# The product with w_out in 2x2 blocks with seven products, and stage weights that arrive one product at a time

## The chip, the cores and the metric

The kernel runs on one core of a Trainium2 chip. A core has five engines that run their own instruction streams: TensorE (PE in the profile; its weight loads are PEld), VectorE (DVE), ScalarE (ACT), GpSimd (POOL) and SyncE (SP), which here only issues DMAs. The metric is the time of one execution in microseconds on the device, as the median of several runs. Before the change it is 1204.18 us (three runs: 1200.9, 1204.18, 1206.41).

## The reference

Three layers run one behind the other on 4608 tokens of width 512:

```
out = softmax(q_c k_c^T / 8) v_c            # attention in chunks of 64, 8 heads
x   = relu(x[mask_e] @ w1[e]) @ w2[e]       # 8 experts, 576 tokens each, greedy routing
h   = max(max(x @ w1, x @ w2), x @ w3)      # last stage: w1, w2, w3 are 512 x 768
y   = h @ w_out                             # w_out is 768 x 512
```

The result is float32. Every matrix product of the last two layers is done in three matmuls, from a high and a low part of each operand: high by high, low weight by high and high weight by low.

## The kernel before

The attention runs first, then routing and the eight experts (one expert after another, 576 tokens each, transposed, so that tokens lie along the free axis), then the last stage. Order on each engine is the order in which the program's lines emit instructions; there is no scheduler behind it. Each engine works through its own list and waits at an instruction until what it reads and overwrites is ready.

The last stage takes the tokens in six blocks of 768 (the loop over `s`). In a block the product with w1, w2, w3 is done in 2x2 blocks of both operands with seven block products (`p1` to `p7`, the loop over `k`, nine groups per block). A block product is six matmuls of 384 columns (`product`), and sums of the 2x2 blocks come before it (`xprep`) and behind it (`best`, which also takes the maximum over the three matrices). The three banks are `px`, `py` and `pz`, two buffers each. The result h is split into a high part by ScalarE and a low part by VectorE (`hpart`, `low`).

Then `layer2` multiplies h by w_out for six tiles of 128 tokens, in the plain way: six parts of the inner dimension by three matmuls of 512 columns, 18 for a tile. Two of these tiles stand between the last products of the block, and `xprep` for the next block stands between the other four. ScalarE copies each tile's result out (`ot`), and GpSimd scatters it to the output rows with an indirect DMA.

The weights of a group lie in DRAM as wda (three products, 768 KB a group) and wdb (four products, 1024 KB). They are loaded whole, two groups at a time in two places each (`wload_a`, `wload_b`), as soon as the last product that uses the place is done. w_out is loaded and split with the experts' weights, as three chunks more at the end of their list (`NC = 8 * E + 3`, `want`). POOL's work in the last stage is the scatter alone.

Of the kernel before, what the change touches and what calls it, by code (L numbers as in the profile page):

```python
# [699 lines left out]
def kernel(ctx, tc, q, k, v, w_gate, w1, w2, m1, m2, m3, m_out, out, mark=lambda n: None):  # L700
# [26 lines left out]
    NC = 8 * E + 3  # L727
# [248 lines left out]
    XO, WA, WB, Y = {}, [], [], []  # L976

    def yload(b):
        for i, tag in enumerate(("aoh", "c64")):
            if b == 0:  # L980
                Y.append(P.tile([128, 2, 2 * TB], F32, name="yraw%d" % i, tag=tag))
            nc.sync.dma_start(Y[i], yd[256 * i:256 * i + 256, b * 2 * TB:(b + 1) * 2 * TB]
                              .rearrange("(a p) t -> p a t", p=128))

    def wload_a(g):
        if g < 9 * NS:
            if g < 2:
                WA.append(P.tile([128, 2, 3, 2, 128], F32R, name="wa%d" % g, tag=("xhi", "xlo")[g]))
            nc.sync.dma_start(WA[g % 2].rearrange("p c o h f -> p (c o h f)").bitcast(F32),
                              wda[g % 9 * 128:g % 9 * 128 + 128].rearrange("p c w -> p (c w)"))  # L990

    def wload_b(g):
        if g < 9 * NS:
            if g < 2:
                WB.append(P.tile([128, 2, 4, 2, 128], F32R, name="wb%d" % g, tag="raw%d" % g))
            nc.sync.dma_start(WB[g % 2].rearrange("p c o h f -> p (c o h f)").bitcast(F32),
                              wdb[g % 9 * 128:g % 9 * 128 + 128].rearrange("p c w -> p (c w)"))

    def xprep(*ops):

        b11, b12 = Y[0][:, :, :TB], Y[0][:, :, TB:]
        b21, b22 = Y[1][:, :, :TB], Y[1][:, :, TB:]
        src = {"b11": b11, "b21": b21, "b22": b22, "t1": T1, "t2": T2, "t3": b12, "t4": b21}
        for o in ops:
            mark("ysplit")
            sub = {"t1": None, "t2": None, "t3": (b22, b12), "t4": (b21, T2)}.get(o)
            if o == "t2":
                nc.vector.tensor_tensor(T1, b12, b11, op=OP.subtract)
                nc.vector.tensor_tensor(T2, b22, T1, op=OP.subtract)
            elif sub:  # L1010
                nc.vector.tensor_tensor(src[o], *sub, op=OP.subtract)
            if o not in XO:
                XO[o] = ring.tile([128, 2, 2, TB], F32R, name="x" + o, tag="chunk")
            nc.scalar.copy(XO[o][:, 0], src[o])
            nc.vector.tensor_tensor(XO[o][:, 1], src[o], XO[o][:, 0].bitcast(F32), op=OP.subtract)
# [9 lines left out]
    for r in range(E):  # L1025
        if r + 1 == E:
            for i in range(3):
                want(mo.rearrange("(a p) f -> p a f", p=128)[:, 2 * i:2 * i + 2, :], 2, 2 * i + 2)
# [6 lines left out]
        for f in range(0, 8, 2):  # L1035
            have(8 * r + f // 2 + 1)
            w = [x.rearrange("p (a f) -> p a f", a=4) for x in chunks[8 * r + f // 2]]
            for f, hf in ((f, 0), (f + 1, 0), (f, 1), (f + 1, 1)) if r + f == 0 else ((f, 0), (f, 1), (f + 1, 0), (f + 1, 1)):
# [26 lines left out]
                if r + 1 == E and not state["next"] and not Y and XH[r][2] == 5:  # L1065
                    yload(0)
# [18 lines left out]
        if r + 1 == E:  # L1085
            while state["next"]:
                convert_one()
            if not Y:
                yload(0)
            for g in range(2):  # L1090
                wload_a(g)
            TMP = P.tile([128, 6, TB], F32, name="tmp", tag="xg")
            T1, T2 = TMP[:, 0:2], TMP[:, 2:4]
        state["l1"] = False
        for d in range(4):
# [20 lines left out]
            if r + 1 == E:  # L1116
                if d == 0:
                    have(NC)
                    for g in range(2):
                        wload_b(g)  # L1120
                xprep(*(("b11", "t2", "b21"), ("t1", "t3"), ("t4",), ("b22",))[d])
# [4 lines left out]
    WO = [x for c in chunks[8 * E:] for x in [[y.rearrange("p (a f) -> p a f", a=2) for y in c]]]  # L1126
    HT = [P.tile([128, 3, 2, 2 * TB], F32R, name="h%d" % i, tag=t) for i, t in enumerate(("hhi", "hlo"))]
    CT = P.tile([128, 2, TB], F32, name="cmax", tag="cw", bufs=2)
    MX = P.tile([128, 2, 2, TB], F32, name="best", tag="pair")
    XB, YZ, U = {}, {}, {}  # L1130
    tt = nc.vector.tensor_tensor
    nct = [0]
    scat = []

    def hview(f):
        return HT[f // 3][:, f % 3]

    def product(g, dst, w, o, x, start, stop):
        mark("mmB")
        n = 0  # L1140
        for dc in range(2):
            for a, c in ((0, 0), (1, 0), (0, 1)):
                nc.tensor.matmul(dst, w[:, dc, o, a], XO[x][:, c, dc], start=start and n == 0, stop=stop and n == 5,  # L1143
                                 skip_group_check=True)
                n += 1

    def best(g, i, j, a, b=None):

        m = g % 3
        M = MX[:, i, j]  # L1150
        if m == 0:
            if b is None:
                nc.scalar.copy(M, a)
            else:
                tt(M, a, b, op=OP.add)
        elif b is None:
            tt(M, M, a, op=OP.max)
        else:
            c = CT[:, nct[0] % 2]
            nct[0] += 1  # L1160
            tt(c, a, b, op=OP.add)
            tt(M, M, c, op=OP.max)  # L1162
        if m == 2:
            nc.scalar.copy(hpart(g, i, j)[0], M)  # L1164

    def hpart(g, i, j):
        h = hview(2 * (g % 9 // 3) + 1 - i)
        return [h[:, x, j * TB:j * TB + TB] for x in range(2)]

    def low(g, i, j):  # L1170
        if g % 3 == 2:
            hi, lo = hpart(g, i, j)
            tt(lo, MX[:, i, j], hi.bitcast(F32), op=OP.subtract)
# [7 lines left out]
    def p6(g):  # L1181
        YZ[g] = [PS.tile([128, 512], F32, name=n)[:, :TB] for n in ("py", "pz")]
        product(g, YZ[g][0], WA[g % 2], 0, "t2", True, False)
# [3 lines left out]
    def p4(g):  # L1187
        product(g, YZ[g][0], WB[g % 2], 0, "t4", False, True)
        best(g, 1, 0, YZ[g][0], U[g, 1])

    def p3(g):
        product(g, YZ[g][1], WB[g % 2], 3, "b22", False, True)
        wload_b(g + 2)
        best(g, 0, 1, YZ[g][1], U[g, 2])

    def p2(g):
        product(g, XB[g], WA[g % 2], 2, "b21", False, True)
        wload_a(g + 2)
        best(g, 0, 0, XB[g])

    def p5(g):
        product(g, YZ[g][1], WB[g % 2], 1, "t1", True, False)

    def p7(g):
        product(g, YZ[g][0], WB[g % 2], 2, "t3", False, False)
        u3 = TMP[:, 4 + g % 2]
        tt(u3, YZ[g][0], U[g, 1], op=OP.add)
        best(g, 1, 1, YZ[g][1], u3)
# [3 lines left out]
    def layer2(t, fs):  # L1212
        if t not in PO:
            PO[t] = PS.tile([128, 512], F32, name="po")
        for f in fs:
            w, h = WO[f // 2], hview(f)
            mark("mmO")
# [3 lines left out]
        if fs[-1] != 5:  # L1221
            return
# [72 lines left out]
```

## Time and profile before

| | |
|---|---|
| runs | 1200.9, 1204.18, 1206.41 us; median 1204.18 |
| profiled execution | 1201.66 us; span in the trace 1199.9 us |
| mean granted TensorE clock | 0.989 of 2.4 GHz; 1.0 throughout the last stage |
| TensorE busy | 1170.7 us, 98% of the span |
| VectorE, ScalarE, GpSimd busy | 828.6, 413.2, 312.3 us |
| last stage | from 653.7 us to the end |

The trace gives, for each instruction, when it started, how long it took, and what the engine waited for before it. Matmuls overlap: one of 384 columns is recorded with 334 ns, but the next starts 173 ns behind it, so the distance between starts is what one costs. The same holds in a small way for VectorE and ScalarE.

### The profile page before, as it was taken

Reading aid. Unit: us, or ns where it says so; the run is one execution under the profiler, and the core shown is the slowest. Engines: PE = TensorE matmul, PEld = TensorE weight load, DVE = VectorE, ACT = ScalarE, POOL = GpSimd, SP = SyncE. Lnnn points to the kernel's source line nnn. Section 1 sums busy time; section 2 is a strip of 40 time slices with the busy share of each in tenths; the row PEclk is TensorE's granted clock in tenths of the full one; section 3 lists DMA queues with packets and bytes.
Section 4 is the critical chain, followed back from the end, with each engine's and each line's share of the span. In section 5 each row is a group of like instructions: output and inputs, shape, how many; then the busy total and the mean of one; then the engine's idle time right before and its main releaser. Section 6 shows DMA issues by size and latency. Waiting matters only on the chain.

```text
span 1199.9 us, 23581 instructions
## 1 busy us (share of the span) xinstructions
PE 1170.7 (98%) x9508; PEld 1095.3 (91%) x9508; DVE 828.6 (69%) x1660; ACT 413.2 (34%) x674; POOL 312.3 (26%) x507
## 2 busy tenths in 40 slices
PE   7999979999999999999999999999999999999998
PEld 5887847999999999999999998998998998998996
DVE  6898976788788888888753665664664664664661
ACT  5998822243333333325333113113113113113111
POOL 8433201011027463757771002002002002002002
PEclk8999978999999999999999999999999999999999
DMA  9999515273646566669755763773773773773651
GB/s 257 274 279 257 159 45 168 89 241 121 210 140 211 181 208 187 196 206 289 240 184 203 288 257 111 288 259 111 286 258 110 287 260 110 288 257 110 237 186 53
DMA packets 138828, 242.99 MB, mean 203 GB/s; under 512 B 30048, under 2 KB 101216, under 8 KB 131808
## 3 DMA queue, kind: packets, MB, share of 16 engines
q1 hardware_dynamic: 118608, 180.90, 46.2%
q0 software_dynamic: 14976, 51.13, 12.8%
q10 hardware_dynamic: 5136, 9.46, 2.3%
q8 instruction: 75, 1.23, 0.4%
q14 instruction: 33, 0.27, 0.1%
HBM read 195.05 MB, written 46.40 MB: 201 GB/s over the span
## 4 chain that ended last, share of the span: by engine, by line
PE 55%; issue 36%; POOL 3%; DVE 3%; SPq 1%; DMA 1%; ACT 1%; POOLq 1%; ACTq 0%; DVEq 0%
PE acc L1105 17%; PE acc L1050 16%; PE pX L181 3%; PE py L1143 2%; PE pT L115 2%; POOL out_dram L1227 2%; PE pS L132 2%; PE po L1219 2%; PE pA L168 2%; PE px L1143 2%; PE pz L1143 2%; PE pxt L821 1%; PE pY L199 1%; PE rp L553 1%; SPq L71 1%
## 5 line engine op out<-in xcount | busy, mean ns | idle before, releaser
L1105 PE MATMUL acc<-hhi,chunk 128*128 128x288 f32 x1024 | 209.9, 299 | 0.0
L1050 PE MATMUL acc<-xhi,chunk 128*128 128x288 f32 (+2 forms) x1024 | 206.4, 300 | 2.5 <-DVE chunk L768 1.3
L1227 POOL DMA_INDIRECT out_dram<-ot,ia x36 | 36.3, 1008 | 508.5 <-ACT ot L1225 507.9
L1050 PEld LDWEIGHTS acc<-xhi,chunk 128*128 128x128 f32 x1024 | 160.7, 188 | 3.7 <-DVE chunk L768 1.5
L1105 PEld LDWEIGHTS acc<-hhi,chunk 128*128 128x128 f32 x1024 | 162.9, 188 | 0.3
L1105 PE MATMUL acc<-hlo,chunk 128*128 128x288 f32 x512 | 150.8, 295 | 0.0
L1219 PE MATMUL po<-chunk,h 128*128 128x512 f32 x648 | 149.3, 390 | 0.0
L1219 PEld LDWEIGHTS po<-chunk,h 128*128 128x128 f32 x648 | 121.4, 188 | 24.8
L1050 PE MATMUL acc<-xlo,chunk 128*128 128x288 f32 (+2 forms) x512 | 143.1, 295 | 0.0
L1143 PE MATMUL px<-xb,wa 128*128 128x384 f32 x648 | 129.9, 334 | 0.7 <-ACT ys L1112 0.7
L1143 PE MATMUL py<-xt,wb 128*128 128x384 f32 x648 | 129.8, 334 | 0.0
L1143 PEld LDWEIGHTS px<-xb,wa 128*128 128x128 f32 x648 | 114.0, 188 | 1.3 <-ACT ys L1112 1.0
L1143 PEld LDWEIGHTS py<-xt,wb 128*128 128x128 f32 x648 | 114.1, 188 | 0.5
L1164 ACT CAST h<-best 128x384 fp32r<-128x384 f32 x72 | 37.0, 514 | 198.1 <-DVE best L1162 121.3
L1105 PEld LDWEIGHTS acc<-hlo,chunk 128*128 128x128 f32 x512 | 96.0, 188 | 0.0
L1050 PEld LDWEIGHTS acc<-xlo,chunk 128*128 128x128 f32 x512 | 93.4, 188 | 0.0
L768 DVE TENSOR_TENSOR chunk<-raw,chunk 128x1024 fp32r<-128x1024 f32 x67 | 86.0, 1289 | 7.6 <-ACT chunk L761 6.6
L1074 ACT ACTIVATE hhi<-acc 128x576 fp32r<-128x576 f32 (+1 forms) x66 | 41.9, 638 | 132.8 <-PE acc L1050 130.1
L798 POOL DMA_INDIRECT xg<-xd,idx x40 | 43.0, 1075 | 167.5 <-DVE ohe L688 88.7
L1179 ACT COPY tmp<-px 128x384 f32<-128x384 f32 x54 | 25.9, 479 | 146.2 <-PE px L1143 146.2
L761 ACT CAST chunk<-raw 128x1024 fp32r<-128x1024 f32 x67 | 69.6, 1046 | 8.6 <-ACT ys L1112 4.8
L1083 DVE SCALAR_TENSOR_TENSOR hlo<-acc,hhi 128x576 fp32r<-128x576 f32 (+1 forms) x66 | 48.3, 735 | 25.3 <-ACT hhi L1074 25.1
(222 smaller groups left out, 2047.9 us busy)
## 6 DMA issues: line engine op xcount, KB each, us to landing
wb<-wdb SPq DMA_DIRECT2D x54, 1024.0 KB
wa<-wda SPq DMA_DIRECT2D x54, 768.0 KB
raw<-in_moe_w_dram SPq DMA_DIRECT2D x64, 512.0 KB
xd<-x POOLq DMA_DIRECT2D x36, 256.0 KB
yd<-ys ACTq DMA_DIRECT2D x32, 288.0 KB
wdb<-pair POOLq DMA_DIRECT2D x18, 512.0 KB
yraw<-yd SPq DMA_DIRECT2D x12, 768.0 KB
ink<-in_k_dram SPq DMA_DIRECT2D x16, 512.0 KB
```

The costliest lines, as they stand in the source:

```text
L181: nc.tensor.matmul(PX[g][c * 64:(c + 1) * 64, hp, :], AT[g][:, hp, c * 64:c * 64 + 64], VB[u % 3][:, 2 * h + c, hp].rearrange("p s i -> p ...
L761: nc.scalar.copy(hi, raw)
L768: nc.vector.tensor_tensor(lo, raw, hi.bitcast(F32), op=OP.subtract)
L798: nc.gpsimd.indirect_dma_start(out=g, out_offset=None, in_=xd[:, :], in_offset=bass.IndirectOffsetOnAxis(ap=rt.idx[r][:, t:t + 1], axis=0))
L1050: nc.tensor.matmul(acc[:, hf, :tk.stop - tk.start], w[a][:, dc, o:o + 128], x[:, dc, tk], start=n == 0, stop=n == 11)
L1074: nc.scalar.activation(hv, src, AF.Relu)
L1083: nc.vector.scalar_tensor_tensor(lv, src, 0.0, hv.bitcast(F32), op0=OP.max, op1=OP.subtract)
L1105: nc.tensor.matmul(acc[:, hf, :288], w[a][:, f, :], x[:, f, tk], start=n == 0, stop=n == 23)
L1143: nc.tensor.matmul(dst, w[:, dc, o, a], XO[x][:, c, dc], start=start and n == 0, stop=stop and n == 5, skip_group_check=True)
L1164: nc.scalar.copy(hpart(g, i, j)[0], M)
L1219: nc.tensor.matmul(PO[t], h[:, x, t % 6 * 128:t % 6 * 128 + 128], w[a][:, f % 2], start=f == 0 and n == 0, stop=f == 5 and n == 2)
L1227: st = nc.gpsimd.indirect_dma_start(out=out, out_offset=bass.IndirectOffsetOnAxis(ap=ia[:, t:t + 1], axis=0), in_=ot, in_offset=None)
```

## The change

The product with w_out gets the same 2x2 form as the product before it. h, at 768 tokens by 768, is cut into four quarters (a11, a12, a22 and a21, which is built in the place of s3), its sums s1 to s4 are formed, and w_out is cut into halves of 256 columns, with sums t1 to t4. A tile is now a pair: 128 tokens of either half of the block. It takes seven products (`o1` to `o7`) of nine matmuls of 256 columns, so 63 for a pair, where two plain tiles took 36 matmuls of 512 columns. There are three pairs in a block, and their parts are put together by VectorE from the banks (`c22`, `c21`, `c12`, and `tt` in `o6` and `o7`) and by ScalarE (`o1`, `o2`).

The splits and sums change engine. In a block 21 halves of h are split instead of 12; the sums are on VectorE, some on GpSimd (`hsum`), most low parts on GpSimd (`low`). The sums and splits of x for the next block (`xsum`, `xsplit`) are on VectorE, except t3, t4 and b22, which are on GpSimd at the end of the block. w_out is no longer in the experts' list; it is loaded, summed and split (`wout`) in the last expert and in the first block.

Weights are loaded product by product, 256 KB in pieces of 1 KB, into eight places (`wload`); the next load for a place is issued when its product is done. Raw x for the next block is loaded into the place of the low half that it later becomes (`yload`).

The main lines of the diff:

```diff
-    NC = 8 * E + 3
+    NC = 8 * E
...
-    def wload_b(g):
-        if g < 9 * NS:
...
+    def wload(n):
+        if n < len(USES):
+            g, o = USES[n]
+            src, o = (wda, o) if o < 3 else (wdb, o - 3)
+            nc.sync.dma_start(WS[n % 8].rearrange("p c h f -> p c (h f)").bitcast(F32),
+                              src[g % 9 * 128:g % 9 * 128 + 128, :, 256 * o:256 * o + 256])
...
+    def xsplit(o, eng):
+        mark("ysplit")
+        nc.scalar.copy(XO[o][:, 0], xraw(o))
+        eng.tensor_tensor(XO[o][:, 1], xraw(o), XO[o][:, 0].bitcast(F32), op=OP.subtract)
...
-    def layer2(t, fs):
-            for n, (a, x) in enumerate(((0, 0), (1, 0), (0, 1))):
-                nc.tensor.matmul(PO[t], h[:, x, t % 6 * 128:t % 6 * 128 + 128], w[a][:, f % 2],
-                                 start=f == 0 and n == 0, stop=f == 5 and n == 2)
+    def outer(t, i, o, n, qs=(0, 1, 2), start=False, stop=False):
+        for q in qs:
+            for m, (a, x) in enumerate(((0, 0), (1, 0), (0, 1))):
+                nc.tensor.matmul(bank(t, i), HB[q, o][x][:, t % 3 * 128:t % 3 * 128 + 128], WQ[q, n, a],
...
+    def o1(t, qs=(0, 1, 2)):
+        outer(t, 0, "a11", 0, qs, start=qs[0] == 0)
+        if qs[-1] == 2:
+            nc.scalar.copy(u(t, 1), bank(t, 0))
...
+                if k % 3 == 0:
+                    hsum(q, dve, "s1", "s2", "s3")
+                    high(q, "s1", "s3", "s2")
+                    low(q, pool, "s1")
...
+        o1(t, (2,))
+        o1(t + 1, (2,))
...
+        o2(t, (0, 1))
+        o2(t + 1, (0, 1))
...
+        o7(t)
+        c22(t)
+        if more:
+            xsum("t1", dve)
+        o7(t + 1)
...
+        scatter(t + 1, 1)
+        pool.drain()
+        t += 2
...
+            xsum("t4", dve)
+            xsplit("t2", dve)
+        o2(t)
+        o7(t)
+        if more:
+            xsplit("b21", dve)
+            xsum("t3", pool)
+        o5(t)
+        c22(t)
+        if more:
+            xsplit("t3", pool)
+            xsplit("t4", pool)
+        o4(t)
+        c21(t)
+        scatter(t, 0)
+        o3(t)
+        c12(t)
+        scatter(t, 1)
+        if more:
+            xsplit("b22", pool)
```

How this moves instructions at the end of a block shows on two engines. First GpSimd, before: from the last scatters of one block to the first of the next there is nothing else in its list (out_0_dram is the output, ot the copied tile, ia the rows' numbers).

```order
L1227 DMA out_0_dram<-ot_10148,ia_2965 4608x512 [waits Activation_49]
L1226 MEMSET wsum_161 1x1 [waits Pool_49]
L1227 DMA out_0_dram<-ot_10173,ia_2965 4608x512 [waits Activation_49]
L1226 MEMSET wsum_161 1x1 [waits Pool_49]
L1227 DMA out_0_dram<-ot_10739,ia_2965 4608x512 [waits DMASW2_49,Activation_49]
```

After, the same place: the third pair's two scatters now stand between splits of x for the next block (hm holds the sums t3 and t4 of x, xt3, xt4 and xb22 are the split operands).

```order
L1309 DMA out_0_dram<-ot3_9504,ia_2965 4608x512 [waits DVE_49,Activation_49]
L1075 TENSOR_TENSOR hm_9238<-xb22_9227,xt3_9225 128x768 [waits DMAHW5_49,DMAHW2_49,DVE_49]
L1080 TENSOR_TENSOR xt3_9225<-hm_9238,xt3_9225 128x768 [waits PE_49,Activation_49]
L1080 TENSOR_TENSOR xt4_9230<-hm_9238,xt4_9230 128x768 [waits PE_49,Activation_49]
L1308 MEMSET wsum_161 1x1
L1309 DMA out_0_dram<-ot_9501,ia_2965 4608x512 [waits DVE_49]
L1308 MEMSET wsum_161 1x1 [waits Pool_49]
L1309 DMA out_0_dram<-ot_9502,ia_2965 4608x512 [waits DVE_49]
L1080 TENSOR_TENSOR xb22_9227<-xb22_9227 128x768 [waits PE_49,Activation_49]
```

GpSimd now has the sum t3, three splits and two scatters in one row, and the split of b22 is the last of them.

Second ScalarE, before, from the last high parts of x to the first two copies of a product of the next block (tmp<-px is the copy of `p1`, on which `p2` waits since it writes on in the same bank).

```order
L1014 CAST xt3_9368<-yraw0_9207 128x768 [waits DVE_49]
L1014 CAST xt4_9424<-yraw1_9209 128x768 [waits DVE_49]
L1225 COPY ot_10148<-po_10129 128x512 [waits DMASW6_49,PE_49,Activation_49]
L1014 CAST xb22_9479<-yraw1_9209 128x768
L1225 COPY ot_10173<-po_10154 128x512 [waits DMASW7_49,PE_49,Activation_49]
L1179 COPY tmp_9244<-px_10177 128x384 [waits PE_49]
L1153 COPY best_9489<-px_10177 128x384 [waits PE_49]
```

After:

```order
L1079 CAST xt3_9225<-hm_9238 128x768 [waits Pool_49]
L1079 CAST xt4_9230<-hm_9238 128x768 [waits DVE_49]
L1079 CAST xb22_9227<-xb22_9227 128x768 [waits DMAHW5_49]
L1254 COPY tmp_9237<-px_10396 128x384 [waits PE_49,Activation_49]
L1241 COPY hm_9238<-px_10396 128x384 [waits PE_49,Pool_49]
```

Before, the first high part waited for VectorE and copies of tiles stood between; now the first waits for GpSimd, which forms t3, and all three and the copy of `p1` stand behind one another.

## Rows read from the trace of the kernel before

**Rows 1.** The page, part 1: busy us, share of the span, instructions, by engine

```profile
PE 1170.7 (98%) x9508; PEld 1095.3 (91%) x9508; DVE 828.6 (69%) x1660; ACT 413.2 (34%) x674; POOL 312.3 (26%) x507
```

**Rows 2.** Waits of TensorE from 650 us on: total us, times, longest

```profile
PE px L1143 <- ACT ys L1112: 0.7, 1, 0.7
```

**Rows 3.** Timeline of TensorE, 715 to 745 us: start, us, engine, line, tile

```profile
715.21 1.20 PE L1143 MATMUL pz<-xt,wb 128*128 128x384 f32 x6
716.25 1.20 PE L1143 MATMUL py<-xt,wb 128*128 128x384 f32 x6
...
722.15 21.96 PE L1219 MATMUL po<-chunk,h 128*128 128x512 f32 x96
743.95 1.23 PE L1143 MATMUL px<-xb,wa 128*128 128x384 f32 x6
```

**Rows 4.** Timeline of TensorE, 193 to 202 us

```profile
195.08 0.64 PE L1050 MATMUL acc<-xlo,chunk 128*128 128x256 f32 x4
195.56 0.60 PE L821 MATMUL pxt<-ident,xg 128*128 128x128 f32 x4
```

**Rows 5.** ScalarE by line and shape from 700 us: busy, mean ns, idle before

```profile
L1179 ACT COPY tmp<-px 128x384 f32<-128x384 f32 x47 | 22.5, 479 | 129.3 <-PE px L1143 129.3
L1225 ACT COPY ot<-po 128x512 f32<-128x512 f32 x36 | 21.1, 586 | 45.1 <-PE po L1219 26.2 <-issue 18.8
L1014 ACT CAST xb<-yraw 128x768 fp32r<-128x768 f32 x15 | 12.6, 837 | 0.0
```

**Rows 6.** VectorE by line and shape from 700 us

```profile
L1162 DVE TENSOR_TENSOR best<-best,cmax 128x384 f32<-128x384 f32 x98 | 54.7, 558 | 3.4
...
L1015 DVE TENSOR_TENSOR xb<-yraw,xb 128x768 fp32r<-128x768 f32 x15 | 14.4, 959 | 17.2 <-ACT xb L1014 17.2
```

**Rows 7.** Timeline of TensorE, 653 to 676 us, first row of the last stage

```profile
653.73 1.31 PE L1143 MATMUL px<-xb,wa 128*128 128x384 f32 x6 [0.73 <-ACT ys L1112]
```

**Rows 8.** Timeline of ScalarE, 600 to 665 us

```profile
653.04 0.64 ACT L1112 COPY ys<-acc 128x576 f32<-128x576 f32 x1 [4.48 <-PE acc L1105]
...
654.08 0.83 ACT L1014 CAST xb<-yraw 128x768 fp32r<-128x768 f32 x1 [0.40 <-ACT ys L1112]
655.13 0.48 ACT L1179 COPY tmp<-px 128x384 f32<-128x384 f32 x1 [0.21 <-PE px L1143]
```

**Rows 9.** Timeline of GpSimd, 629 to 634.5 us, with VectorE idle

```profile
632.07 0.74 POOL L878 TENSOR_TENSOR pair<-cw,pair 128x256 fp32r<-128x256 f32 x1
...
633.13 0.46 POOL L878 TENSOR_TENSOR pair<-cw,pair 128x128 fp32r<-128x128 f32 x1
```

**Rows 10.** Timeline of GpSimd, 595 to 602 us

```profile
598.73 1.78 POOL L878 TENSOR_TENSOR pair<-cw,pair 128x256 fp32r<-128x256 f32 x1
600.46 0.86 POOL L877 CAST pair<-cw 128x256 fp32r<-128x256 f32 x1
```

**Rows 11.** Timeline of VectorE, 595 to 602 us

```profile
598.68 1.22 DVE L768 TENSOR_TENSOR chunk<-raw,chunk 128x1024 fp32r<-128x1024 f32 x1 [3.46 <-ACT chunk L761]
599.83 1.23 DVE L919 SCALAR_TENSOR_TENSOR c<-c 128x512 f32<-128x512 uint32 x1
```

**Rows 12.** Timeline of GpSimd, 1020 to 1205 us: the scatters of one block

```profile
1087.87 0.97 POOL L1227 DMA_INDIRECT out_dram<-ot,ia  x1 [71.35 <-ACT ot L1225]
...
1089.23 0.97 POOL L1227 DMA_INDIRECT out_dram<-ot,ia  x1 [0.30 <-ACT ot L1225]
...
1100.51 0.09 POOL L1226 MEMSET wsum<- 1x1 f32 x1 [2.10 <-issue]
```

**Rows 13.** Windows: us, busy PE, PEld, DVE, ACT, POOL, clock, DMA share, GB/s

```profile
285.60:290.80 5.20, 5.20 (x42) 5.13 (x41) 4.30 (x12) 0.65 (x1) 0.00 (x0) 1.00 0.97 305
657.00:713.00 56.00, 56.00 (x325) 56.00 (x324) 34.60 (x64) 8.99 (x19) 0.00 (x0) 1.00 0.73 272
```

**Rows 14.** DMA of the window 285.6 to 290.8 us

```profile
DMA packets 1583, 1.59 MB, mean 305 GB/s; under 512 B 47, under 2 KB 1582, under 8 KB 1582
```

**Rows 15.** The page, part 5: splits of the weight chunks

```profile
L768 DVE TENSOR_TENSOR chunk<-raw,chunk 128x1024 fp32r<-128x1024 f32 x67 | 86.0, 1289 | 7.6 <-ACT chunk L761 6.6
L761 ACT CAST chunk<-raw 128x1024 fp32r<-128x1024 f32 x67 | 69.6, 1046 | 8.6 <-ACT ys L1112 4.8
```

More of the change, by code (lines that the diff above doesn't have):

```diff
@@ L992, in wload_b @@
-    def wload_b(g):
[L993 to L1015, printed above, removed]
@@ L1087 @@
                 convert_one()
[L1088 to L1093, printed above, removed]
+            have(NC)
+            homes()
+            yload(0, "b11", "t3", "b21", "b22")
+            for n in range(8):
+                wload(n)
+            wout(0, "load")
+            dve, pool = nc.vector, nc.gpsimd
         state["l1"] = False
@@ L1117 @@
                 if d == 0:
[L1118 to L1121, printed above, removed]
+                    xsum("t1", dve)
+                    xsplit("b11", dve)
+                    xsum("t2", dve)
+                    xsplit("t1", dve)
+                elif d == 1:
+                    xsum("t4", dve)
+                    xsplit("t2", dve)
+                    xsplit("b21", dve)
+                    wout(0, "sums")
+                elif d == 2:
+                    xsum("t3", dve)
+                    xsplit("t3", dve)
+                    xsplit("t4", dve)
+                    wout(0, range(3))
+                else:
+                    xsplit("b22", dve)
+                    wout(0, range(3, 7))
@@ L1124 @@
     c3.close()
     PS = ctx.enter_context(tc.tile_pool(name="bps", bufs=2, space=PSUM))
[L1126 to L1129, printed above, removed]
+    blocks()
+    TMP = FP["u"][:, :5 * TB].rearrange("p (n t) -> p n t", n=5)
@@ L1155, in best @@
                 tt(M, a, b, op=OP.add)
-        elif b is None:
+        else:
+            if b is not None:
+                tt(b, a, b, op=OP.add)
+                a = b
             tt(M, M, a, op=OP.max)
[L1158 to L1173, printed above, removed]
     def p1(g):
         XB[g] = PS.tile([128, 512], F32, name="px")[:, :TB]
-        product(g, XB[g], WA[g % 2], 1, "b11", True, False)
+        product(g, XB[g], "b11", True, False)
         U[g, 1] = TMP[:, g % 2]
@@ L1253 @@
+        more = s + 1 < NS
+        t = 3 * s
+        if more:
+            yload(s + 1, "b11", "b21", "t3")
+        o1(t, (0, 1))
+        o6(t, (0, 1))
         p4(g)
-        low(g, 1, 0)
+        hsum(2, dve, "s1", "s2", "s3")
+        high(2, "s1", "s2", "s3")
+        low(2, dve, "a11")
         p3(g)
-        low(g, 0, 1)
-        low(g, 1, 1)
-        layer2(t + 1, (0, 1, 2, 3))
-        layer2(t, (4, 5))
-        layer2(t + 1, (4, 5))
-        more = s + 1 < NS
-        for i in range(2, 6):
-            if i == 4:
-                nc.gpsimd.drain()
-            if more:
-                xprep(*(("b11", "t2"), ("b21", "t1"), ("t3", "t4"), ("b22",))[i - 2])
-            layer2(t + i, (0, 1, 2, 3, 4, 5))
+        if more:
+            yload(s + 1, "b22")
@@ new lines @@
+        o7(t)
+        c22(t)
+        if more:
+            xsum("t1", dve)
+        o7(t + 1)
+        c22(t + 1)
+        if more:
+            xsplit("b11", dve)
+        o4(t)
+        c21(t)
+        scatter(t, 0)
+        o4(t + 1)
+        c21(t + 1)
+        scatter(t + 1, 0)
+        if more:
+            xsum("t2", dve)
+            xsplit("t1", dve)
+        o3(t)
+        c12(t)
+        scatter(t, 1)
+        o3(t + 1)
+        c12(t + 1)
+        scatter(t + 1, 1)
+        pool.drain()
@@ new lines @@
+        t += 2
+        o1(t)
+        o6(t)
+        if more:
+            xsum("t4", dve)
+            xsplit("t2", dve)
+        o2(t)
+        o7(t)
+        if more:
+            xsplit("b21", dve)
+            xsum("t3", pool)
+        o5(t)
+        c22(t)
+        if more:
+            xsplit("t3", pool)
+            xsplit("t4", pool)
+        o4(t)
+        c21(t)
+        scatter(t, 0)
+        o3(t)
+        c12(t)
+        scatter(t, 1)
+        if more:
+            xsplit("b22", pool)
```

254 lines of the change are left out of this document (194 added, 60 removed).

## The prediction, made before the changed kernel was run

> **What bounds the kernel now.** I read the page's totals first, then TensorE's waits, then its timeline in the last stage, then the other engines' rows there, then the DMA windows. TensorE is busy for 98% of the span [rows 1]. From 650 us on, where the whole change lies, it waits once, for 0.7 us, on its first matmul [rows 2, 7]. So in the last stage every microsecond is matmul issue, and the distance between starts is the price. Six matmuls of 384 columns start 1.04 us after the six before them, 173.4 ns each; 96 of 512 columns take 743.95 - 722.15 = 21.80 us, 227.1 ns each [rows 3]. VectorE has slack there (34.6 of 56 us busy) [rows 13], ScalarE more, GpSimd only scatters. The change thus takes work from the one engine that is full and gives it to others. It gains what the matmuls lose, as long as the others stay in time.
>
> **The matmuls.** Before, a block of 768 tokens takes 6 tiles x 18 = 108 matmuls of 512 columns: 108 x 0.2271 = 24.53 us. After, 3 pairs x 7 products x 9 = 189 of 256 columns. The kernel before has such a matmul in its first expert: four of them start 0.48 us ahead of the next work, 120 ns each [rows 4]. 189 x 0.120 = 22.68 us. The gain is 1.85 us a block and 11.1 us in six blocks. Counting multiplications alone it would be an eighth, 18.4 us; the rest goes to the fixed part of a matmul, about 13 ns beyond columns at the full clock (120 against 106.7), of which there are now 81 more in a block. The 42 x 54 matmuls of the earlier product stay as they are.
>
> The Trainium skill, "TensorE: Matmul & The Clock Gate", section "Back-to-back issue gap", gives columns / 2.4 + 2.5 ns for a warm, isolated matmul. By that page's figure 256 columns would cost 109 ns and 512 columns 216 ns, and the gain would be 16.0 us, an estimate. The rows say 120 and 227, with weight loads between, so the trace disagrees by 11 ns on each matmul, and the gain is the smaller one.
>
> **Waits within the product with w_out.** A group of six in `px` that starts at 653.73 is recorded to 655.04, and ScalarE copies at 655.13 [rows 7, 8]; so 0.09 us behind the recorded end. Four matmuls of 256 columns are recorded for 0.64 us and cost 0.48 [rows 4]: the recorded end lies 0.16 behind the next start. A copy of 256 columns I extrapolate from 479 ns for 384 and 586 for 512 to 372 ns [rows 5], and TensorE starts 0.05 behind a copy's end (653.68 to 653.73) [rows 7, 8]. `o2` of the first pair goes on in the bank that `o1` has just left, so it must wait 0.09 + 0.16 + 0.37 + 0.05 = 0.67 us; only `o1` of the second pair's last third (3 x 0.12 = 0.36) covers it. That leaves 0.31 us, six times: 1.9 us. Bounds: 0 if the copy comes out ahead, 0.67 x 6 = 4.0 if nothing covers.
>
> `o4` of the second pair waits for VectorE's third sum of that pair, which stands behind `xsum("t1")`, 0.96 us long [rows 6]. I take 0.2 us in each of five blocks, 1.0 us; bounds 0 and 0.96 x 5 = 4.8.
>
> **The end of a block.** Here most is added, and to GpSimd and ScalarE. Call T the end of the block's last product. The third pair's seven products take 7 x 1.08 = 7.56 us. GpSimd's scatters start 1.36 us apart, and the `drain` leaves it idle for 2.10 us [rows 12]. The first scatter needs `c21` of the first pair. VectorE comes to it late: the second pair's `o7` ends at T - 7.56 - 4 x 1.08 = T - 11.9, and then it has the rest of `xsum("t1")`, the third sum and `c22` of that pair (0.42 each, from 558 ns for 384 columns and 959 for 768) [rows 6], the split of b11 (0.96) and `c21` itself, some 2.7 us: T - 9.1. Four scatters end at T - 9.1 + 3 x 1.36 + 0.97 = T - 4.0, and the drain at T - 1.9. Then GpSimd forms t3 on 768 columns. No row shows that; 128 columns take 0.46 us and 256 take 0.74 [rows 9], so 0.28 for 128 more, and 0.46 + 5 x 0.28 = 1.86 us. t3 is there at about T + 0.1.
>
> ScalarE then does the high parts of t3, t4 and b22 (0.84 us each [rows 5], which I take 0.75 apart from start to start, as the two engines overlap a little) and behind them the copy of `p1` (0.48): it ends at about T + 2.9. `p2` stands behind `p1` and `p6` and could start at T + 2.08. It waits 0.85 us. On GpSimd the split of t3 starts at T + 1.0, t4 follows, then two scatters, then b22: 1.0 + 1.86 + 1.86 + 2 x 1.36 + 1.86 = T + 9.3. `p3` of the first group needs b22 behind eight products, at T + 8.3, or T + 9.2 with the wait just found. Both chains ask for about the same delay, so I take 0.85 once for a boundary, five times: 4.3 us. t3 and t4 themselves are in time (needed at T + 4.2 and T + 7.3, there at T + 2.9 and T + 4.7). Bounds: 0 if GpSimd is 1 us quicker than that; and if a VectorE instruction of 0.96 us holds up each of the four, 3.8 more a boundary, so 23 us in all.
>
> **The first block.** ScalarE's copy of the last expert ends at 653.68, and b22's high part runs to 654.9 [rows 8]. Behind it now stand two high parts of w_out of 512 columns, and GpSimd splits what they read (0.46 + 3 x 0.28 = 1.30 us for the first). The copy of `p1` overwrites these sums, so it waits until about 656.8 and ends at 657.3; `p2` could start at 655.8. 1.5 us, once; bounds 0 and 2.8 (both splits).
>
> **What costs nothing.** In the groups VectorE gets three sums of 0.56 us every third group and loses the splits of h, which GpSimd takes: eight instructions of 0.46 + 2 x 0.28 = 1.02 us in 22 us. The banks are double, so a result may be late by over 1 us before TensorE sees it. If that cover is gone, it is the second rival. The three chunks less in the last expert save splits of 1.05 and 1.29 us each [rows 15] on engines that TensorE didn't wait for. At the end a VectorE sum of 256 columns (0.42) replaces a copy of 0.59: -0.2 us.
>
> **The loads.** A product's 256 KB now come in 1 KB pieces. In the window from 285.6 us nearly all packets are of that size (1582 of 1583 under 2 KB) [rows 14], and 305 GB/s came at a DMA share of 0.97 [rows 13]. 262 KB at 305 GB/s take 0.86 us, and a product lasts 1.04: the engines would be some 80% full, where the groups before had 0.73 at 272 GB/s. With seven products of lead (7.3 us) I count no wait.
>
> **The sum.** -11.1 + 1.9 + 1.0 + 4.3 + 1.5 - 0.2 = -2.6 us. Against the profiled execution (1201.66 us; span 1199.9) that is 1199.1; against the median of the runs shown, 2.5 us higher, 1201.6. So my forecast is no change that can be told: a measurement of this kernel tells 0.5%, 6 us, from no change.
>
> **Rivals.**
> Covers hold (chance 0.33): GpSimd and ScalarE come in time at the boundary, and only the waits in the banks stay, or not even these. The gain is between 11.3 and 6: at best 1204.18 - 11.3 = 1192.9 us. For it: each wait found is under 1 us, and a drain shorter by 1 us removes the boundary's. Against it: GpSimd's time on 768 columns is an extrapolation with no slack in it.
>
> GpSimd late at the boundary (0.18): its split of b22 holds `p3`. GpSimd and VectorE hinder each other: a GpSimd instruction that takes 0.74 us alone took 1.78 while VectorE ran one on two SBUF operands, and the next VectorE one took 1.23 us [rows 10, 11]. The changed kernel runs such pairs all through the stage, where GpSimd had nothing to do before. If each of GpSimd's four instructions loses 0.96 us so, five boundaries cost 19 us more: 1201.6 + 19 = 1220.6. It is slower by over 6 us from 0.45 us more on each of these instructions, 2.3 us instead of 1.86. Against it: VectorE's instructions at T and behind it read a bank, not two SBUF tiles, but for the split of b21.
> The Trainium skill, "SBUF — State Buffer", section "Who interferes with whom", has this as an exclusive lock: of VectorE with two SBUF inputs and a GpSimd instruction, the second waits until the first is through. The trace agrees (1.78 us is 0.74 and most of 1.22).
>
> Loads too slow (0.02): at 200 GB/s a product's load takes 1.31 us, 0.27 more than the product. 63 products make 17 us, less about 4 of lead, six times: 78 us, 1280. For it: pieces of 1 KB where a group's rows were 6 and 8 KB long (768 and 1024 KB over 128 partitions). Against it: the 305 GB/s above.
>
> That leaves 0.47 for the forecast. **Chances and range.** Faster by over 0.5%: 0.33, the first rival. Within 0.5%: 0.47. Slower: 0.20, the second and third. The forecast's own range is 1198 to 1208. The whole takes in the first rival to its end, 1193, and the second to about a third of its price, 1213.
>
> **What the profile of the changed kernel would show.** Matmuls of 256 columns 120 ns apart, and a block's product with w_out 22.7 us without waits. Five waits of `px` for ScalarE's copy just behind the first two products of a block, 0.5 to 1.2 us each, and none or small ones of `pz` for GpSimd's split of b22; six of 0.3 us before `o2`; none for a weight load. GpSimd's instructions of 768 columns at 1.9 us. I am wrong if the waits on GpSimd's b22 are over 2 us a block, if TensorE waits for loads, if 256 columns cost other than 120 ns, or if the end of a block shows no wait at all.

## The result, and the profile after

The changed kernel takes 1211.04 us (median of 7 runs, 1209.44 to 1212.45) against 1204.18 (7 runs): 1.0057 times the kernel before, 95% interval 1.0040 to 1.0074. It is slower by 6.9 us. The forecast was 1201.6, no change that can be told.

| | before | after |
|---|---|---|
| profiled execution; its span, us | 1201.66; 1199.9 | 1212.45; 1210.6 |
| first matmul of the last stage | 653.73 | 656.22 |
| from there to the stage's last matmul | 540.66 | 548.27 |
| from the last matmul's start to the end | 5.5 | 6.1 |

The 2.5 us ahead of the last stage belong to no edit: they are there already at the first matmul of the first expert (194.02 and 196.50), ahead of all that the change moves. The last expert, in which the work on w_out now begins, takes 51.76 us in all eleven profiles of this study, in which the last stage starts at 653.3 to 658.9. Stages are therefore compared from their first matmul to their last. Here that is +7.6 us.

Part 1 of the page after the change, which answers to [rows 1]: TensorE is busy for 3.9 us less in a span that is 10.7 longer, so it stands idle; GpSimd is busy for 178 us more.

```profile
PE 1166.8 (96%) x9994; PEld 1112.2 (92%) x9994; DVE 852.8 (70%) x1745; ACT 432.2 (36%) x738; POOL 490.6 (41%) x660
```

What TensorE waits for from 650 us on (total us, times, longest), to be read against [rows 2]:

```profile
PE px L1215 <- ACT tmp L1254: 12.0, 6, 3.8
PE px L1215 <- ACT ys L1173: 0.7, 1, 0.7
```

Six waits stand for the copy of `p1` (`tmp<-px`): one in the first block, five at the ends of blocks. None is for a load, none for b22. The timeline of TensorE shows the size of a matmul and the first two ends of a block:

```profile
744.22 0.52 PE L1294 MATMUL pz<-wo,hbhhi 128*128 128x256 f32 x3
744.58 0.52 PE L1294 MATMUL pz<-wq,hbhlo 128*128 128x256 f32 x3
...
747.42 1.21 PE L1215 MATMUL px<-xb,ws 128*128 128x384 f32 x6
748.47 1.20 PE L1215 MATMUL py<-xt,ws 128*128 128x384 f32 x6
753.49 2.29 PE L1215 MATMUL px<-xb,ws 128*128 128x384 f32 x6 [3.82 <-ACT tmp L1254]
755.57 2.12 PE L1215 MATMUL pz<-xt,ws 128*128 128x384 f32 x6
...
842.66 1.21 PE L1215 MATMUL px<-xb,ws 128*128 128x384 f32 x6
843.71 1.20 PE L1215 MATMUL py<-xt,ws 128*128 128x384 f32 x6
846.49 1.31 PE L1215 MATMUL px<-xb,ws 128*128 128x384 f32 x6 [1.58 <-ACT tmp L1254]
```

Three matmuls of 256 columns are 0.355 us apart, 118.3 ns each, where [rows 4] gave 120. At the first end of a block `p2` starts at 753.49, though `p6` started at 748.47 and takes 1.04: 3.98 us are lost. Behind it six matmuls take 2.08 instead of 1.04. At the second 1.74 are lost. (The brackets give less, since they count from the recorded end of the matmul before.) The windows show the clock there (us, busy PE, PEld, DVE, ACT, POOL, granted clock, DMA share, GB/s); the last row is the window of [rows 13]:

```profile
749.52:753.49 3.97, 0.15 (x2) 0.01 (x1) 0.03 (x1) 2.67 (x4) 3.03 (x3) 0.83 0.48 132
753.50:759.20 5.70, 5.70 (x18) 5.70 (x19) 0.52 (x1) 0.48 (x1) 5.31 (x6) 0.52 0.37 119
657.00:713.00 56.00, 54.49 (x311) 53.40 (x310) 33.69 (x59) 17.13 (x38) 32.19 (x33) 1.00 0.81 256
```

During the wait the granted clock fell to the lower level, 1.2 GHz, at 752.1, and it stayed there until 759.0, 5.5 us behind the start of `p2`; 0.83 and 0.52 are the means of the two windows.

GpSimd sets the moment. Its timeline at the first two ends of a block, the fourth scatter, the sum t3 (`hm<-xb,xt`, in brackets the idle time before it) and the splits; at the second also the first two scatters:

```profile
743.25 1.23 POOL L1309 DMA_INDIRECT out_dram<-ot,ia  x1 [0.22 <-issue]
748.91 1.81 POOL L1075 TENSOR_TENSOR hm<-xb,xt 128x768 f32<-128x768 f32 x1 [4.44 <-PE px L1215]
...
833.77 1.78 POOL L1309 DMA_INDIRECT out_dram<-ot,ia  x1 [6.29 <-DVE ot L1345]
...
835.85 0.97 POOL L1309 DMA_INDIRECT out_dram<-ot,ia  x1 [0.21 <-issue]
...
838.40 1.32 POOL L1309 DMA_INDIRECT out_dram<-ot,ia  x1 [0.22 <-issue]
841.89 1.83 POOL L1075 TENSOR_TENSOR hm<-xb,xt 128x768 f32<-128x768 f32 x1 [2.17 <-PE py L1294]
844.67 3.60 POOL L1080 TENSOR_TENSOR xt<-hm,xt 128x768 fp32r<-128x768 f32 x2 [0.95 <-ACT xt L1079]
```

VectorE beside the first scatter, and ScalarE behind t3 (three high parts, then the copy of `p1`):

```profile
833.40 0.41 DVE L1345 TENSOR_TENSOR ot<-po,tmp 128x256 f32<-128x256 f32 x1
833.74 0.95 DVE L1075 TENSOR_TENSOR hm<-xb,hm 128x768 f32<-128x768 f32 x1
```

```profile
843.76 1.57 ACT L1079 CAST xt<-hm 128x768 fp32r<-128x768 f32 x2 [3.98 <-POOL hm L1075]
845.23 0.83 ACT L1079 CAST xb<-xb 128x768 fp32r<-128x768 f32 x1
845.97 0.47 ACT L1254 COPY tmp<-px 128x384 f32<-128x384 f32 x1
```

T, the end of the block's last product, is 842.66. The chain is unbroken: scatters to 839.72, drain to 841.89, t3 to T + 1.06, high parts, copy to 846.44, `p2` at 846.49. A scatter takes 0.97 us alone [rows 12]; the first took 1.78 with VectorE's sum of two SBUF tiles beside it and a split of two more (834.60, 0.95 us) right behind that, and the fourth 1.32.

The account of the last stage, from the distances between all its matmuls:

| term, us | predicted | measured |
|---|---|---|
| matmuls: 648 x 227.1 to 1134 x 118.3 ns | -11.1 | -13.0 |
| first block | 1.5 | 2.5 |
| `o2` behind ScalarE's copy, six times | 1.9 | 2.2 |
| `o4` behind VectorE's third sum, five times | 1.0 | 1.6 |
| ends of five blocks | 4.3 | 14.3 |
| behind the last matmul | -0.2 | 0.6 |
| sum | -2.6 | 8.2 |

### The profile page after: what moved, and what is told of

It reads as the page before. It is cut to its first block, busy times and chain, and to the rows that moved or that the text cites. A ratio compares the mean times of both kernels' runs of the same rounds, so it can differ in the third digit from the quotient of the medians.

```text
span 1210.6 us, 25836 instructions
## 1 busy us (share of the span) xinstructions
PE 1166.8 (96%) x9994; PEld 1112.2 (92%) x9994; DVE 852.8 (70%) x1745; ACT 432.2 (36%) x738; POOL 490.6 (41%) x660
## 4 chain that ended last, share of the span: by engine, by line
PE 86%; DVE 4%; issue 3%; ACT 2%; POOL 2%; SPq 1%; DMA 1%; POOLq 0%; ACTq 0%; DVEq 0%
PE acc L1166 17%; PE acc L1112 16%; PE py L1215 14%; PE pz L1215 9%; PE px L1215 9%; PE pX L181 3%; PE px L1294 2%; PE pT L115 2%; PE py L1294 2%; PE pS L132 2%; PE pA L168 2%; PE po L1294 2%; PE pxt L821 1%; PE pY L199 1%; PE pz L1294 1%
## 5 line engine op out<-in xcount | busy, mean ns | idle before, releaser
L1215 PE MATMUL py<-xt,ws 128*128 128x384 f32 x972 | 188.1, 335 | 0.0
L1215 PEld LDWEIGHTS py<-xt,ws 128*128 128x128 f32 x972 | 170.6, 189 | 0.6 <-DVE tmp L1280 0.6
L1215 PE MATMUL px<-xb,ws 128*128 128x384 f32 x648 | 131.6, 337 | 12.7 <-ACT tmp L1254 12.0
L1215 PEld LDWEIGHTS px<-xb,ws 128*128 128x128 f32 x648 | 114.0, 189 | 15.0 <-ACT tmp L1254 13.9
L768 DVE TENSOR_TENSOR chunk<-raw,chunk 128x1024 fp32r<-128x1024 f32 x64 | 80.6, 1265 | 5.7 <-ACT chunk L761 5.6
L1280 DVE TENSOR_TENSOR tmp<-py,tmp 128x384 f32<-128x384 f32 x54 | 30.1, 557 | 72.7 <-PE py L1215 72.6
L1260 DVE TENSOR_TENSOR tmp<-py,tmp 128x384 f32<-128x384 f32 x54 | 30.1, 558 | 64.3 <-ACT tmp L1254 48.9
L761 ACT CAST chunk<-raw 128x1024 fp32r<-128x1024 f32 x64 | 66.6, 1047 | 8.0 <-ACT ys L1173 6.4
L1254 ACT COPY tmp<-px 128x384 f32<-128x384 f32 x54 | 25.8, 479 | 119.4 <-PE px L1215 118.3
L1215 PE MATMUL pz<-xt,ws 128*128 128x384 f32 x324 | 65.8, 338 | 0.0
L1215 PE MATMUL pz<-xb,ws 128*128 128x384 f32 x324 | 64.8, 334 | 0.0
```

The lines of the kernel that those rows point to most:

```text
L761: nc.scalar.copy(hi, raw)
L768: nc.vector.tensor_tensor(lo, raw, hi.bitcast(F32), op=OP.subtract)
L1215: nc.tensor.matmul(dst, w[:, dc, a], XO[x][:, c, dc], start=start and n == 0, stop=stop and n == 5, skip_group_check=True)
L1260: tt(U[g, 2], YZ[g][0], U[g, 1], op=OP.add)
```

## The experiments

Each kernel ran in turns with the kernel before on the same chip. "Stage" is the time from the first matmul of the last stage to its last.

| kernel | median, us | kernel before | ratio (95%) | stage, us |
|---|---|---|---|---|
| changed kernel, once more | 1212.01 | 1203.32 | 1.0072 (1.0051 to 1.0094) | 548.73 |
| drain last | 1204.37 | 1201.87 | 1.0013 (0.9997 to 1.0030) | 540.72 |
| t3 on VectorE | 1201.29 | 1201.87 | 0.9993 (0.9980 to 1.0007) | 537.68 |
| no t2 | 1206.03 | 1201.87 | 1.0032 (1.0017 to 1.0047) | 543.24 |
| b22 behind the copy | 1208.28 | 1203.32 | 1.0043 (1.0026 to 1.0060) | 544.64 |
| loads alone | 1217.52 | 1201.87 | 1.0141 (1.0109 to 1.0172) | 554.39 |
| loads alone, x at the end | 1202.56 | 1203.32 | 0.9997 (0.9982 to 1.0011) | 540.66 |
| combined | 1196.18 | 1203.32 | 0.9936 (0.9914 to 0.9958) | 533.47 |
| combined, two edits more | 1192.52 | 1202.30 | 0.9908 (0.9887 to 0.9929) | 528.98 |

**The drain last.**

```diff
         scatter(t + 1, 1)
-        pool.drain()
...
         if more:
             xsplit("b22", pool)
+        pool.drain()
```

> Edit: GpSimd's drain goes from behind the fourth scatter of a block to behind the split of b22, the last thing GpSimd does in the block. In the changed kernel, at a later boundary, the fourth scatter ends 2.94 us before T (T is the end of the block's last product), GpSimd is idle for 2.17 us, its sum t3 ends at T + 1.06 and p2 waits 1.85 us; the first boundary has an idle time of 4.44 us and a wait of 3.98 us, followed by some 5.7 us at half clock. My theory (the chain scatters, drain, t3, three high parts, copy of p1): t3 comes 2.1 us earlier at each boundary and the five waits go, 14.2 us: 1211.0 - 14.2 = 1196.8. Rival 1 (GpSimd and VectorE hold each other up): t3 then falls beside VectorE's split of b21 and its other sums with two SBUF operands and grows by about 0.95; 0.8 us of each wait stay, 1200.8. Rival 2 for the first boundary alone: if its longer idle time is not the drain's but a transfer's, the wait of about 4 us and the half clock stay there, and 7.8 us go, 1203.2.

The stage lost 7.5 us, not 14.2. All five waits of `p2` at the ends of blocks went, the first included (one is left, in the first block), so the longer idle time there was the drain's. But a new wait of 1.28 us came at five places, the rival's mechanism through another door. TensorE's waits, and TensorE, GpSimd and VectorE at the second end of a block:

```profile
PE pz L1294 <- DVE ot L1339: 5.6, 5, 1.1
PE px L1215 <- ACT tmp L1254: 1.5, 1, 1.5
```

```profile
835.25 0.62 PE L1294 MATMUL pz<-wo,hbhlo 128*128 128x256 f32 x3 [1.12 <-DVE ot L1339]
```

```profile
832.20 1.84 POOL L1075 TENSOR_TENSOR hm<-xb,xt 128x768 f32<-128x768 f32 x1
```

```profile
832.37 2.48 DVE L1080 TENSOR_TENSOR xb<-xb 128x768 fp32r<-128x768 f32 x1
834.78 0.41 DVE L1339 TENSOR_TENSOR ot<-pz,tmp 128x256 f32<-128x256 f32 x1
```

t3 did not grow (1.84 us); VectorE's split of b21 beside it did, from 0.95 to 2.48. It started 0.17 us later and ended 0.81 us behind t3's end, so it got through only when t3 was done. `c22` stands behind it on VectorE, and `o3` waits for `c22`. The rival had the right cause and the wrong victim.

**The sum t3 on VectorE.**

```diff
             xsplit("b21", dve)
-            xsum("t3", pool)
+            xsum("t3", dve)
```

> Edit: the sum t3 at the end of a block goes from GpSimd to VectorE, at the same place of the program (behind VectorE's split of b21). VectorE is idle for 5.4 us behind T in the changed kernel. My theory: t3 is there about 1 us before T, the three high parts are done before the copy of p1, and the five waits of p2 go (14.2 us); c22 of the third pair comes 0.95 later on VectorE and o3 waits for it some 0.6 us, five times 3 us: 1211.0 - 11.2 = 1199.8. Rival (what holds p2 is ScalarE, whose three high parts of 0.84 us are simply one too many): waits of 1 us or more stay at each boundary, 1205 or more.

As my theory had it: the waits of `p2` went, and the expected wait for `c22` came, 0.61 us five times (the view's 0.5 leaves out the part hidden by the recorded ends). ScalarE's three high parts are no bound by themselves. Of the waits for the copy of `p1`, only that of the first block is left.

```profile
PE pz L1294 <- DVE ot L1339: 2.3, 5, 0.5
PE px L1215 <- ACT tmp L1254: 1.5, 1, 1.5
```

**No t2.**

```diff
         scatter(t + 1, 0)
-        if more:
-            xsum("t2", dve)
-            xsplit("t1", dve)
         o3(t)
```

> Edit: the sum t2 and the split of t1 are left out at the end of a block (so the next block multiplies with the t1 of the first block and with what lies in t2's place). These two VectorE instructions read two SBUF tiles, run for 0.95 us each, and the first runs beside the first scatter, which takes 1.78 us instead of 0.97. If VectorE's instruction is what lengthens the scatter, the first scatter takes 0.97, t3 ends 0.8 to 1.2 us earlier and p2's wait falls from 1.85 to 0.65 to 1.05 us at four boundaries; with the first boundary that is 4 to 6 us: 1205 to 1207. If the scatter is long for another reason (the first of a row, for instance), it stays at 1.78 and the time stays at 1211. If that lengthening is off the path, the scatter shrinks and the time stays.

The stage lost 5.0 us. GpSimd at the first two ends of a block:

```profile
739.59 0.97 POOL L1309 DMA_INDIRECT out_dram<-ot,ia  x1 [0.21 <-ACT xt L1079]
745.98 1.81 POOL L1075 TENSOR_TENSOR hm<-xb,xt 128x768 f32<-128x768 f32 x1 [5.42 <-PE px L1215]
...
829.78 0.98 POOL L1309 DMA_INDIRECT out_dram<-ot,ia  x1 [6.28 <-DVE ot L1345]
...
833.60 0.97 POOL L1309 DMA_INDIRECT out_dram<-ot,ia  x1 [0.21 <-issue]
836.75 1.93 POOL L1075 TENSOR_TENSOR hm<-xb,xt 128x768 f32<-128x768 f32 x1 [2.17 <-PE pz L1294]
```

The first scatter takes 0.98: the two VectorE instructions had lengthened it. The fourth takes 0.97; it now starts ahead of VectorE's sum of t4 (833.60 against 833.94), in the changed kernel behind its start. The four later waits fell from 1.74, 2.01, 1.79 and 1.76 to 0.67, 1.28, 0.68 and 0.68, near what I had predicted for all five (0.85). The Trainium skill, "SBUF — State Buffer", section "Who interferes with whom", has an exclusive lock between VectorE with two SBUF inputs and a GpSimd instruction that reads SBUF; the runs agree for sums and splits (0.95 to 2.48 us above). The same section infers that a `tensor_tensor`, the kind of VectorE's sums and splits here, leaves the issue of a DMA on GpSimd alone; this trace shows a scatter lengthened all the same (1.78 us beside two of them, 0.98 without), which decides. Whether that is because a scatter also reads its rows' numbers from SBUF is open.

The first end of a block did not follow: the scatters ended earlier, the idle time grew to 5.42, and the wait stayed at 3.89. So there something else ends last; the next run takes it up.

**The changed kernel once more.**

> The changed kernel as it is, beside the next three kernels on the same chip: 1.0057 times the kernel before if its first comparison holds. What the repetition can tell: the idle time of GpSimd behind the drain was 4.44 us at the first boundary and 2.2 at the others. If that belongs to the place in the program, the same 4.4 stand here, with 4 us of wait and TensorE at its lower clock behind it; if it was an accident of one execution, about 2.2 us and a wait of 1.85 stand at the first boundary too, and the stage is some 4.5 us shorter in this profile.

The first wait is 3.97 us again, at the lower clock behind it again. It belongs to the program. What the transfers did is read from the first profile of the changed kernel: the DMA view of the first end of a block (2.5 us from 744.5, behind the fourth scatter) and of the second (2.4 us from 839.6), each digit a fortieth:

```profile
DMA  0900000019697796975000001001001000000000
...
q0 software_dynamic: 81, 0.26, 26.7%
q8 instruction: 1, 0.02, 2.3%
```

```profile
DMA  0000000000089699988986000000000000000000
...
q0 software_dynamic: 80, 0.26, 26.8%
```

At the second end the scatter's packets are through at 840.9, and t3 starts 1.0 us later. At the first a transfer of instructions (q8, 16 KB) lies in front, and single packets of the scatter come as late as 746.4. So the idle time there, 2.3 us longer, has two parts: the packets end 0.7 later, and t3 starts 2.5 us behind the last of them, 1.5 more than at the second end.

In all eleven profiles the drain's own record ends with the transfers and not with the scatter instruction: 0.6 to 0.7 us behind the scatters' last packet at every later end of a block (0.9 at one), and 2.0 to 2.4 behind it at the first. So the 1.5 us belong to the first drain of the stage in every kernel here; why is open. That the transfer of instructions makes the packets late is argued and not shown: where it took 1.54 us ("no t2") and not 0.92, the idle time was 5.42 and not 4.44, but no run takes it away. The kernel before has the longer first drain too (3.52 against 2.10 in [rows 12]), with no transfer on q8 beside it and nothing that waited for it:

```profile
741.39 0.09 POOL L1226 MEMSET wsum<- 1x1 f32 x1 [3.52 <-issue]
```

**b22 behind the copy of `p1`.**

```diff
         scatter(t, 1)
-        if more:
-            xsplit("b22", pool)
...
             p1(g)
+            if s and k == 0:
+                xsplit("b22", pool)
```

> Edit: in the changed kernel ScalarE's high part of b22 (0.83 us) and GpSimd's split of it stand behind the first product of the next block and its copy, instead of ahead of it. If the chain drain, t3, high parts, copy of p1 sets the wait link by link, each boundary's wait falls by 0.73 to 0.83 us (1.85 to about 1.05; the first from 4.0 to 3.2): 4 us less than the changed kernel. If it is the drain alone and the order on ScalarE doesn't matter, nothing changes. If GpSimd's split of b22 comes late for p3 by that, new waits of pz stand seven products later.

Each wait fell by 0.72 to 0.99 us, so ScalarE's order is a link of the chain. The first end gained 3.2 us, since no low clock followed its wait any more (timeline of TensorE, then windows), the four others 3.3 together. New waits of `p3` for b22, 0.2 us and a slow matmul at each end, took 1.5 back, one product of the last block 0.8, by a wait whose cause is open, and small gaps the rest.

```profile
751.98 1.32 PE L1215 MATMUL px<-xb,ws 128*128 128x384 f32 x6 [3.06 <-ACT tmp L1254]
753.15 1.21 PE L1215 MATMUL pz<-xt,ws 128*128 128x384 f32 x6
```

```profile
748.80:751.97 3.17, 0.12 (x1) 0.00 (x0) 0.01 (x1) 1.98 (x4) 2.23 (x2) 1.00 0.55 165
752.00:757.70 5.70, 5.70 (x33) 5.70 (x34) 1.75 (x4) 1.62 (x3) 5.30 (x7) 1.00 0.41 131
```

**The loads alone**, in the kernel before; the edit puts `wload` and `product` of the change in place of `wload_a` and `wload_b`.

> Edit: the kernel before, with only the loads of the changed one: each product's 256 KB come by themselves in rows of 1 KB into eight places, in the order of use, instead of whole groups (768 and 1024 KB) into two places each. My theory: they cost nothing, TensorE never waits for them: 1204.2 within 2 us, and the DMA share in the groups rises from 0.73 to about 0.8. Rival (the loads take part of what the product with w_out gained, as waits or as slower matmuls): 1206 or more, with waits of px, py or pz for a transfer.

A miss: 15.6 us slower. TensorE's waits; SyncE's queue and TensorE around the first of them:

```profile
PE py L1142 <- DMA ws<-wda: 10.9, 5, 3.0
```

```profile
666.85 1.28 SPq L982 DMA_DIRECT2D yraw<-yd  x2
668.23 0.53 SPq L994 DMA_DIRECT2D ws<-wda  x1
```

```profile
676.05 2.35 PE L1142 MATMUL py<-xt,ws 128*128 128x384 f32 x12 [1.55 <-DMA ws<-wda]
```

The kernel before issues the next block's x (1.5 MB) in the second group of a block. In one queue with loads that lead by eight products it holds the weights up. The edit was thus not the change's part alone: the change also moves the x load.

**The loads alone, x at the end.**

```diff
-            if k == 1 and s + 1 < NS:
-                yload(s + 1)
         t = 6 * s
+        if s + 1 < NS:
+            yload(s + 1)
```

> Edit: the kernel before with the loads of the changed one (each product by itself, eight places), as in the run with the loads alone, and the load of the next block's x (1.5 MB) goes from behind the second group of a block to its end, where the changed kernel has it. In the run with the loads alone five waits of 1.7 to 3.1 us for a weight load stood one group behind the x load, 11.8 us in all, one of them with some 2 us at the lower clock behind it, and 1217.5 against 1201.9 was measured. If the x load in the same queue is their cause, they all go and the time is that of the kernel before within 2 us. If loads product by product are too slow by themselves, waits of the same size stay elsewhere in the groups, 1210 or more.

No wait for a load, and the time of the kernel before. Waits from 650 us on, and the window of [rows 13]:

```profile
PE px L1142 <- ACT ys L1108: 0.7, 1, 0.7
```

```profile
657.00:713.00 56.00, 56.00 (x325) 56.00 (x324) 34.46 (x65) 8.98 (x19) 0.00 (x0) 1.00 0.82 252
```

Loads product by product cost nothing, as the prediction said, provided nothing large comes between them while the products run.

**Combined.** The core of the edits:

```diff
         c22(t)
-        if more:
-            xsum("t1", dve)
         o7(t + 1)
         c22(t + 1)
         if more:
-            xsplit("b11", dve)
+            xsum("t1", dve)
...
+        o5(t, (2,))
         o2(t, (0, 1))
...
             xsplit("b21", dve)
-            xsum("t3", pool)
         o5(t)
         c22(t)
         if more:
+            xsum("t3", dve)
             xsplit("t3", pool)
```

> The changed kernel with five edits of order and place: the drain as the last thing of a block on GpSimd; the sum t3 on VectorE, behind c22 of the third pair; the last third of o5 of the first pair ahead of o2; the sum t1 behind the third sum of the second pair; w_out's first sums where the copy of p1 doesn't overwrite them, and their splits behind that copy. My theory: the waits at the five boundaries, before o2 and before o4 go, and that of the first block falls from 1.77 to about 0.4. The last stage then has 2268 x 173.4 + 1134 x 118.3 ns = 527.4 us of matmuls and about 1.5 of waits, 529 us from its first matmul to its last against 548.3 in the changed kernel: 19 us less, 1192, faster than the kernel before by 0.8 to 1.1%. Rival (the two engines hold each other up wherever sums of x are put): a wait of 0.5 to 1.3 us stays in each block, as in the run with the drain last, 1195 to 1199.

The stage is 533.5 us, not 529, and the ratio 0.9936. The waits for t3, before `o2`, before `o4` and in the first block went; which of the five edits took which was not tried one by one. In their place `o5`, now earlier, waited 0.40 us in each block for VectorE's low part of s1, `p2` still 0.28 five times, and one product of the last block 0.8. The time lies in the rival's range, but not by its mechanism: scatters still grow beside VectorE (to 1.48 and 1.74 us), but nothing waits for them, and VectorE's instructions ahead of `o5` take their usual 0.55 us. The waits that are left come from the order on VectorE and ScalarE, as the next run shows.

**Combined, two edits more.**

```diff
+        low(2, dve, "s1")
         p3(g)
...
-        low(2, dve, "s1")
...
             p1(g)
+            elif k == 0:
+                xsplit("b22", pool)
+                pool.drain()
```

> The combined version with two edits more, each aimed at a wait that its trace still shows: VectorE's low part of s1 comes ahead of the last p3's maximum (o5 of the first pair waited 0.40 us for it in each of six blocks), and the high part and split of b22, with the drain behind them, come behind the first product of the next block and its copy (p2 still waited 0.28 us at five boundaries). If each wait is paid for one to one and nothing else is late next, 2.4 + 0.9 us go: about 530 us from the first matmul of the last stage to its last, and 1193. If the low part of a12, now 0.5 us later, holds o2 or o6 in their place, 1195 to 1196 as before.

Both waits were paid for one to one (2.4 and 1.4 us), and the 0.8 us of the last block went too, though no edit aimed at it: the stage is 528.98 us. That leaves 1.6 us of gaps in 527.4 us of matmuls. In the view of waits only the one that the kernel before has too is left, and the first end of a block is closed:

```profile
PE px L1214 <- ACT ys L1173: 0.7, 1, 0.7
```

```profile
747.70 1.21 PE L1214 MATMUL px<-xb,ws 128*128 128x384 f32 x6
748.75 1.20 PE L1214 MATMUL py<-xt,ws 128*128 128x384 f32 x6
749.79 1.20 PE L1214 MATMUL px<-xb,ws 128*128 128x384 f32 x6
```

At 0.9908 (0.9887 to 0.9929) of the kernel before this version beats both.

## Why the prediction was wrong

The step that failed is the end of a block: "I take 0.85 once for a boundary, five times: 4.3 us". It measured 14.3. The mechanism was the one named, `p2` behind the copy of `p1`, behind three high parts, behind t3; two links and what followed were mis-sized.

First, "Four scatters end at T - 9.1 + 3 x 1.36 + 0.97 = T - 4.0": they ended at T - 2.94, since the first took 1.78 and the fourth 1.32. A bound for such a hold-up stood in the text ("if a VectorE instruction of 0.96 us holds up each of the four"), but the rival "GpSimd late at the boundary" shows that it was meant for GpSimd's four instructions of 768 columns ("2.3 us instead of 1.86"). These kept 1.80 to 1.86 us; for the scatters I took such a hold-up as nothing. The order on VectorE, with a sum of two SBUF tiles right behind the two `c21`, would have shown that at least the first scatter is hit. My argument against the lock looked at T and later; the scatters lie ahead of T. Without those two instructions the later waits are 0.67 to 1.28: the price is 0.7 to 1.1 us at each of four ends. (By its own terms the text's t3 ends at T, not T + 0.1; that slip is small beside this.)

Second, the drain. I took 2.10 us from a later block [rows 12]; in the first block it was 4.44, and longer still when the scatters ended earlier. It ended there some 1.3 us behind T, not 1.9 ahead of it, and made the first wait 3.98 instead of 0.85. The trace of the kernel before has the long first drain too (3.52); I had read only a later one.

Third, TensorE's lower clock behind that wait, some 2.6 us, had no place in the sum.

Right by the runs: 768 columns on GpSimd take 1.83 us (1.86 extrapolated), the copy of 256 columns 0.373 (0.372); `p3` never waited for b22; the loads cost nothing at a DMA share of 0.81 (some 80% predicted). Too small: the gain of the matmuls (118.3 ns, not 120), the wait before `o4` (0.31 for 0.2 each), that before `o2` (0.37 for 0.31) and the first block (a wait of 1.67 us and 0.85 in small gaps). The term behind the last matmul had the wrong sign (0.6 for -0.2); two scatters now follow each other there, 1.57 us apart. The 109 ns that the prediction worked out, as an estimate, from the Trainium skill, "TensorE: Matmul & The Clock Gate", section "Back-to-back issue gap", stay further off than the 120. The rival "GpSimd late at the boundary" had the engine and the lock, but put them on b22 and on the splits; t3 and the scatters ahead of it were what came late.

## What to carry to other kernels

Where the end of a stage hangs on a chain over several engines, walk the chain with the lengthened times, not those of an engine alone: list beside each GpSimd instruction the VectorE instructions with two SBUF inputs that the program puts there. A drain belongs behind the last thing that anyone waits for. A change that gains on the full engine can lose it all in orders and places: the same seven products gave 1.0057 here, and 0.9908 with sums, a drain and splits moved.

## What the runs showed of the hardware that was not expected

- GpSimd and VectorE with two SBUF inputs held each other up by who came first where both did sums or splits: a VectorE split grew from 0.95 to 2.48 us beside a GpSimd sum of 1.84 that started 0.17 us ahead. With scatters it went one way only. Over the eleven profiles a scatter took 1.07 to 1.81 us where a VectorE instruction of 768 columns with two SBUF inputs was running when it began (once 0.98), and 0.96 to 1.03 elsewhere; no scatter lengthened such a VectorE instruction (0.95 to 0.96, once 1.02).
- A drain on GpSimd left it idle for 2.2 to 2.5 us at the later ends of a block in the changed kernel, but for 4.44 (5.42 without t2) at the first. It ended 0.6 to 0.7 us behind the last packet of the scatters, and at the first one of the stage 2.0 to 2.4 behind it, in all eleven profiles.
- TensorE's clock behind waits, by the rows: with 3.98 us lost before `p2` it was at the lower level for 5.5 us behind the wait; with 3.89 ("no t2"), for 3.2; with 3.23 ("b22 behind the copy"), not at all. The length of one wait does not settle it: in "loads alone" one of 3.07 us had 3.4 us at the lower level shortly behind it, and one of 3.13 had none.
